# Sparse attention followed by a Fourier mix, one core: three of the four parts of a block sum added by the transfers

## The chip, the cores and the metric

The kernel runs on one core of one Trainium2 chip. Times are device microseconds of a whole execution. A profile is one further execution, recorded instruction by instruction; its span runs from the first to the last instruction, and a little of the execution's own time lies around it.

## The reference

There are 4 batches of 768 positions. The first half is an attention of 8 heads with 64 columns, in which a position looks at its neighbours closer than 16 positions and at 24 summaries, one for each block of 32 positions. The second half takes the attention's output, 512 columns wide, through a Fourier mix and a feed-forward of 2048 columns.

```python
k_sum = k.reshape(B, H, nb, block, D).max(axis=3)          # block = 32, nb = 24
v_sum = v.reshape(B, H, nb, block, D).mean(axis=3)         # the block sums of this case
scores = concat(where(|i - j| < 16, scale * q @ k.T, -1e9),
                scale * q @ k_sum.T + log(block))
x = softmax(scores) @ concat(v, v_sum)                     # then (B, S, H * D)
u = x + real(fft(fft(x, axis=1), axis=2))                  # over positions, then columns
un = (u - mean(u)) / sqrt(var(u) + 1e-6)
out = u + relu(un @ w_ch1) @ w_ch2
```

## The kernel before

**Stages.** All batches go through attention, Fourier mix and the two products with w_ch1 and w_ch2. Batch 0's attention stands alone at the start (`first_attention`, an order written out by hand for TensorE and VectorE). After it come batch 0's Fourier mix and normalisation, batch 1's attention and the conversion of the weights, interleaved by `drive`, which advances several generators in turn. The weights arrive as 64-bit floating point words and are turned into 32-bit ones by `convert` (lines 1096 to 1116: an exponent and a mantissa part, with two steps on ScalarE between VectorE's), and `make` adds the sums that the later products need. From about 80 us on, the hidden products of batch 0 run (`gen_hidden`, lines 1377 to 1410), each in pieces named hx, hy and hz whose results VectorE and ScalarE gather into h.

**The order.** Outside the hand-written part, a scheduler orders each engine's instructions by its own estimate of when they become ready, by the priorities that `drive` passes along and by `issue_after` marks. The order is fixed in the built program: each engine works through its own list, and an instruction that has to wait holds up all behind it. SyncE issues the plain transfers (`fetch`) and, through eight semaphores used in turn, each of its transfers waits until the eighth before it has landed.

**The block sums.** `block_sums(b, gg)` prepares the sums of four heads: 4 x 24 = 96 rows, one for each head and block, of 32 positions x 64 columns. For batches after the first, a row is loaded in four pieces of 8 positions, 96 x 512 values or 192 KB each, into four buffers `vb`. `add_later_blocks` adds the four pieces together; then, for batch 1, one reduction over the 8 positions that are left gives `vbs` (96 x 64). `scale_sums` multiplies it on TensorE with a table that picks the rows (vs, line 817), for two heads at a time. Batch 1 does the additions on VectorE (`tt`), later batches on GpSimd (`gtt`).

For the first four heads of batch 1, (b, gg) = (1, 0), the loads are issued in `finish_pair`, inside the hand-written part, and the additions stand behind it:

```python
            if g == NP - 2:
                block_sums(1, 0)
                load(1, 1)
...
    with tc.manual_schedule(engines={mybir.EngineType.PE, mybir.EngineType.DVE}):
        first_attention()
    add_later_blocks(1, 0)
```

**Names that follow.** qk (line 726) are the transposed keys and queries of batch 1, sc the scores with the neighbours (793), ss with the block maxima km (811, km made at 700), p the exponentials (800), av the products with the values (829, 834). x<-mx (571) adds the Fourier mix to x, bst and both (1306, 1307) are its statistics, norm (1319 to 1331) the square roots, big or un the normalised rows (1276, 1279), unt their transposes (1349), u their copies with the sums that the products need. Line 571 is the helper `tt` of nearly all of VectorE's additions, line 551 that of `fetch`, line 574 that of `gtt`. `turned` and `xr` (958, 959) are the only transfers that GpSimd issues; they belong to the Fourier mix of the last two batches.

Of the kernel before, what the change touches and what calls it, by code (L numbers as in the profile page):

```python
# [488 lines left out]
def _main_program(ctx, tc, q, k, v, moe_w_ch1, moe_w_ch2, out):  # L489


    nc = tc.nc
# [19 lines left out]
    ADD, SUB = ALU.add, ALU.subtract  # L512
# [36 lines left out]
    def fetch(out, in_):  # L549

        ins = nc.sync.dma_start(out=out, in_=in_)
        if in_order[0]:
            tc.keep_in_program_order(ins)
        return ins.ins
# [18 lines left out]
    def gtt(out, in0, in1, op):  # L573
        return nc.gpsimd.tensor_tensor(out=out, in0=in0, in1=in1, op=op).ins
# [25 lines left out]
    def room(name):  # L600
        return bpool.tile([P, NC * 2 * S], FP, tag="room", name=name)
# [12 lines left out]
    def block_sums(b, gg):  # L614

        heads, rows = slice(4 * gg, 4 * gg + 4), 4 * nb
        f = BLOCK // 4
        n = f * D
        vb = spool.tile([rows, D], FP, tag="vbs", bufs=2, name=f"vbs_{b}_{gg}")
        for g in (2 * gg, 2 * gg + 1):  # L620
            sums[b, g] = vb, sel[:, g % 2]
        src = v[b, heads].rearrange("h (n f) d -> (h n) (f d)", f=BLOCK)
        if b == 0:

            raw = words[0:rows, 4 * n * gg:4 * n * (gg + 1)]
            fetch(out=raw, in_=src)
            to_add[gg] = raw, vb
            return
        if done_weights:
            raw = room(f"vb_{b}_{gg}")  # L630
            raw = [raw[0:rows, n * i:n * (i + 1)] for i in range(4)]
        else:

            raw = [bpool.tile([P, NC, P], FP, tag="s", bufs=5, name=f"vb_{b}_{gg}_{i}").rearrange("p n t -> p (n t)")
                   [0:rows] for i in range(4)]
        for i in range(4):
            fetch(out=raw[i], in_=src[:, n * i:n * (i + 1)])
        to_add[b, gg] = raw, vb
        if (b, gg) != (1, 0):
            add_later_blocks(b, gg)  # L640

    def add_later_blocks(b, gg):
        f = BLOCK // 4
        raw, vb = to_add[b, gg]
        add = gtt if b > 1 else tt
        add(raw[0], raw[0], raw[1], ADD)
        add(raw[2], raw[2], raw[3], ADD)
        add(raw[0], raw[0], raw[2], ADD)
        if b == 1:
            nc.vector.tensor_reduce(out=vb, in_=raw[0].rearrange("p (f d) -> p d f", d=D), op=ADD, axis=AX.X)  # L650
            return
        while f > 2:
            f //= 2
            gtt(raw[0][:, 0:f * D], raw[0][:, 0:f * D], raw[0][:, f * D:2 * f * D], ADD)
        gtt(vb, raw[0][:, 0:D], raw[0][:, D:2 * D], ADD)
# [195 lines left out]
    def first_attention():  # L851
# [8 lines left out]
        def finish_pair(g):  # L860
            wide_values(0, g, p[g], x)
# [3 lines that stand above are left out]
            load_values(*following(0, g, 2))  # L865
# [125 lines left out]
    def gen_attention(b):  # L991
# [6 lines left out]
        if b > 1:  # L998
            yield
            yield  # L1000
            with tc.issue_after(marks["load"]):
                block_sums(b, 0)
            for _ in range(2):
                yield
        for g in range(NP + 1):
# [33 lines left out]
            if g == 1 and b > 1:  # L1039
                block_sums(b, 1)  # L1040
# [467 lines left out]
    for vw in vw_bufs:  # L1508
        nc.gpsimd.tensor_copy(out=vw[:, :, D].rearrange("p (e n) -> p e n", e=2),
                              in_=count[:, None, :].to_broadcast([P, 2, NQ]))  # L1510
# [26 lines left out]
# [3 lines that stand above are left out]
    fetch(out=near, in_=dr["near"].ap().rearrange("p (h i) c -> p h i c", h=2))  # L1540
    fetch(out=half_of, in_=dr["half"].ap())
# [92 lines left out]
```

## Time and profile before

| | us |
|---|---|
| three runs: median, lowest, highest | 793.76, 792.52, 799.07 |
| the profiled execution | 790.53 |
| its span | 788.6 |
| TensorE busy in the span | 776.1 |
| VectorE busy in the span | 491.2 |
| ScalarE, GpSimd busy | 224.1, 49.2 |

The granted TensorE clock of the profiled execution is 0.999 on average. A row of a timeline gives the start in us from the span's start, the time in us from the first start to the last end, the engine (PE is TensorE, DVE VectorE, ACT ScalarE, POOL GpSimd), the line, the operation, what it writes and reads, the shapes, how many instructions are merged in the row, and in brackets how long the engine had stood idle before it and what ended that. Instructions that follow each other on an engine overlap a little, so the distance from one start to the next is what a row costs. A row of a table by stretches gives the stretch, its length, the busy time with the number of instructions, the granted clock, the DMA engines' busy share and the GB/s moved. A DMA share may pass 1, since a packet's time counts where it starts.

### The profile page before, as it was taken

The page shows a single profiled execution, that of the slowest core. Times are in us where ns is not written, and L with a number is a line of the kernel's source. Part 1 is how long each engine was busy: PE and PEld are TensorE (multiplying, and loading weights), DVE is VectorE, ACT ScalarE, POOL GpSimd, SP SyncE. Part 2 cuts the span into 40 slices and gives each one's busy share as a digit, 9 for nine tenths or more (in the row PEclk, how much of TensorE's full clock was granted, in tenths as well). Part 3 has the DMA queues.
Part 4 walks back from the last instruction along what each step waited for, and adds up shares of the span by engine and source line. Part 5 has one row for each costly group of instructions (what it writes and reads, how often), then busy time and mean ns, then how long its engine had stood idle before and what let it go on. Part 6 is the DMA issues. An engine that isn't in the chain of part 4 may idle for free.

```text
span 788.6 us, 14351 instructions
## 1 busy us (share of the span) xinstructions
PE 776.1 (98%) x5920; PEld 562.9 (71%) x5920; DVE 491.2 (62%) x1017; ACT 224.1 (28%) x491; POOL 49.2 (6%) x87
## 2 busy tenths in 40 slices
PE   9999999999999999999999999999999999999997
PEld 6778455445588866787578866788569865886686
DVE  5899978697889566652759545552667623533352
ACT  3565656236536022100236012200136012001200
POOL 0000000000000030200310020300220000000000
PEclk9999999999999999999999999999999999999999
DMA  9999887796855279965442169611513163106001
GB/s 214 184 266 237 206 275 196 242 260 221 232 161 155 49 231 261 204 103 177 154 144 87 54 209 212 184 55 31 223 44 134 54 220 134 47 0 234 0 28 57
DMA packets 133353, 121.82 MB, mean 154 GB/s; under 512 B 94464, under 2 KB 114912, under 8 KB 133088
## 3 DMA queue, kind: packets, MB, share of 16 engines
q1 hardware_dynamic: 132160, 118.53, 53.9%
q0 software_dynamic: 576, 2.10, 0.8%
q8 instruction: 48, 0.79, 0.4%
q10 hardware_dynamic: 544, 0.20, 0.1%
q14 instruction: 25, 0.20, 0.1%
HBM read 97.22 MB, written 23.59 MB: 153 GB/s over the span
## 4 chain that ended last, share of the span: by engine, by line
PE 87%; DVE 9%; ACT 1%; issue 1%; DMA 1%; POOL 0%; SPq 0%; DVEq 0%; POOLq 0%
PE hx L1377 19%; PE ox L1446 18%; PE hz L1377 10%; PE oz L1446 9%; PE hy L1377 5%; PE oy L1446 5%; PE o L1423 4%; PE y L1258 3%; PE sc L793 2%; PE mx L1217 2%; PE av L829 1%; PE av L834 1%; PE qk L718 1%; DVE x L571 1%; PE unt L1349 1%
## 5 line engine op out<-in xcount | busy, mean ns | idle before, releaser
L1377 PE MATMUL hx<-u,w 128*128 128x384 f32 x512 | 185.4, 491 | 1.5 <-ACT h L1394 0.7
L1377 PEld LDWEIGHTS hx<-u,w 128*128 128x128 f32 x512 | 94.9, 190 | 70.3 <-ACT p L800 3.8
L1377 PE MATMUL hz<-u,w 128*128 128x384 f32 x256 | 93.7, 487 | 0.2 <-DVE u L571 0.2
L1446 PE MATMUL oz<-w,s 128*128 128x256 f32 x336 | 81.3, 380 | 0.0
L1446 PE MATMUL ox<-w,s 128*128 128x256 f32 x336 | 80.1, 380 | 0.0
L1446 PE MATMUL ox<-w,h 128*128 128x256 f32 x336 | 79.6, 381 | 0.0
L571 DVE TENSOR_TENSOR x<-ox,x 128x256 f32<-128x256 f32 x84 | 35.5, 423 | 66.2 <-PE ox L1446 65.9
L1377 PEld LDWEIGHTS hz<-u,w 128*128 128x128 f32 x256 | 48.4, 190 | 34.1 <-DVE u L571 0.8
L1446 PEld LDWEIGHTS ox<-w,h 128*128 128x128 f32 x336 | 63.1, 190 | 10.8 <-issue 1.2
L1446 PEld LDWEIGHTS oz<-w,s 128*128 128x128 f32 x336 | 63.3, 190 | 8.9 <-DVE x L571 0.4
L1446 PEld LDWEIGHTS ox<-w,s 128*128 128x128 f32 x336 | 63.2, 190 | 9.0 <-DVE x L571 0.3
L1388 ACT COPY h<-hx 128x384 f32<-128x384 f32 x32 | 15.3, 479 | 187.1 <-PE hx L1377 187.1
L571 DVE TENSOR_TENSOR h<-hy,h 128x384 f32<-128x384 f32 x32 | 17.8, 557 | 48.4 <-PE hy L1377 48.2
L1377 PE MATMUL hy<-u,w 128*128 128x384 f32 x128 | 46.8, 487 | 0.6 <-DVE h L571 0.6
L571 DVE TENSOR_TENSOR h<-hx,h 128x384 f32<-128x384 f32 x32 | 17.8, 556 | 44.1 <-PE hx L1377 43.9
L1423 PE MATMUL o<-w,h 128*128 128x512 f32 x96 | 42.3, 595 | 0.7 <-DVE w L571 0.7
L1407 ACT ACTIVATE h<-hx 128x384 f32<-128x384 f32 x32 | 15.7, 490 | 88.3 <-PE hx L1377 88.2
L1446 PE MATMUL oy<-w,h 128*128 128x256 f32 x168 | 40.1, 380 | 0.0
L571 DVE TENSOR_TENSOR x<-oz,x 128x256 f32<-128x256 f32 x42 | 17.8, 424 | 30.4 <-PE oz L1446 30.1
L1377 PEld LDWEIGHTS hy<-u,w 128*128 128x128 f32 x128 | 24.1, 190 | 16.9 <-DVE h L571 0.7
L1446 PEld LDWEIGHTS oy<-w,h 128*128 128x128 f32 x168 | 31.8, 190 | 4.4
L1423 PEld LDWEIGHTS o<-w,h 128*128 128x128 f32 x96 | 18.0, 190 | 22.7 <-issue 20.7
(167 smaller groups left out, 1072.8 us busy)
## 6 DMA issues: line engine op xcount, KB each, us to landing
w<-dw SPq DMA_DIRECT2D x44, 896.0 KB, 5.7
words<-in_moe_w_ch_dram SPq DMA_DIRECT2D x32, 512.0 KB, 5.7
dw<-w SPq DMA_DIRECT2D x12, 896.0 KB, 7.5
vw<-in_v_dram SPq DMA_DIRECT2D x47, 192.0 KB, 6.1
out_dram<-x SPq DMA_DIRECT2D x23, 256.0 KB, 2.0
vb<-in_v_dram SPq DMA_DIRECT2D x24, 192.0 KB, 6.8
kn<-in_k_dram SPq DMA_DIRECT2D x9, 384.0 KB, 6.1
qn<-in_q_dram SPq DMA_DIRECT2D x9, 384.0 KB, 7.6
```

The costliest lines, as they stand in the source:

```text
L571: return nc.vector.tensor_tensor(out=out, in0=in0, in1=in1, op=op).ins
L718: nc.tensor.matmul(ps[D * e:D * (e + 1), s:S2:HT], src[:, e, h, s, :], ident, start=True, stop=True)
L793: ins = nc.tensor.matmul(ps[h][r:r + 64, i, :], kt[rows, o:o + 64], qt[rows, o:o + BLOCK], start=True, stop=True)
L829: nc.tensor.matmul(av[r][32 * j:32 * (j + 1), t, :], p[rows, h, i - NB2 * h, :], vw[rows, i, :], start=(t == 0), stop=False, skip_group_ch ...
L834: ins = nc.tensor.matmul(av[r][:, t:t + HT + 1:HT, :], pm[rows, P * t:P * (t + 1)], vs[rows], start=False, stop=(t == HT - 1), skip_group_ ...
L1217: nc.tensor.matmul(out, y[:, g], table, start=False, stop=True, skip_group_check=True)
L1258: nc.tensor.matmul(y, fgs[b][par][:, st, P * g:P * (g + 1)], fs[par][:, g % 2, st, :], start=(st == 0), stop=(st == n - 1))
L1377: ins = nc.tensor.matmul(ps, w[:, a, kk, :], u[:, r, kk, :], start=start and kk == 0, stop=stop and kk == 1, skip_group_check=True)
L1388: nc.scalar.copy(out=c11, in_=X)
L1407: nc.scalar.activation(out=c21, in_=X, func=AF.Relu)
L1423: nc.tensor.matmul(ps, h[:, n, hf, P * t:P * (t + 1)], wt[2, b, j][:, 2 * hf:2 * hf + 2, :], start=(n, hf) == (0, 0), stop=(n, hf) == (NC ...
L1446: nc.tensor.matmul(ps, left[a][:, n, :], wt[2, b, j][:, r, :], start=start and n == 0, stop=stop and n == NC - 1, skip_group_check=True)
```

## The change

For (b, gg) = (1, 0) alone, SyncE loads only the first piece. The other three are transfers issued by GpSimd that add their values onto the first buffer (`accum_op=ADD`), and `add_later_blocks` leaves out the three additions; the reduction stays on VectorE. Each of the three transfers waits for the one before. All other block sums stay as they were.

```diff
-        for i in range(4):
-            fetch(out=raw[i], in_=src[:, n * i:n * (i + 1)])
+        if (b, gg) == (1, 0):
+            fetch(out=raw[0], in_=src[:, 0:n])
+            for i in range(1, 4):
+                nc.gpsimd.dma_start(out=raw[0], in_=src[:, n * i:n * (i + 1)], accum_op=ADD)
+        else:
+            for i in range(4):
+                fetch(out=raw[i], in_=src[:, n * i:n * (i + 1)])
...
-        add(raw[0], raw[0], raw[1], ADD)
-        add(raw[2], raw[2], raw[3], ADD)
-        add(raw[0], raw[0], raw[2], ADD)
+        if (b, gg) != (1, 0):
+            add(raw[0], raw[0], raw[1], ADD)
+            add(raw[2], raw[2], raw[3], ADD)
+            add(raw[0], raw[0], raw[2], ADD)
```

## The prediction

> **What bounds the kernel now.** First the head of the page, then TensorE's busy time in 20 us stretches, to see how much idle time there is to win and where.
>
> ```profile
> span 788.6 us, 14351 instructions
> PE 776.1 (98%) x5920; PEld 562.9 (71%) x5920; DVE 491.2 (62%) x1017; ACT 224.1 (28%) x491; POOL 49.2 (6%) x87
> ...
> 60.00:80.00 20.00, 19.05 (x388) 1.00 1.02 242
> 80.00:100.00 20.00, 18.69 (x216) 1.00 0.86 212
> 100.00:120.00 20.00, 20.00 (x113) 1.00 0.84 265
> ```
>
> TensorE is the bound. From 60 to 240 us its busy time falls 4.34 us short of the clock, after 240 us by about 0.4 us up to the tail. In 60 to 100 us, the only stretch where the added block sums can matter, 2.26 us are missing (0.95 + 1.31). So no relief of VectorE brings more than about 4 us, half a per cent; a loss has no such ceiling.
>
> Then VectorE's timeline where the three additions stand, with the rows around them:
>
> ```profile
> 53.25 0.70 DVE L1096 TENSOR_SCALAR words<-words 128x1024 int32<-128x1024 int32 x1 [0.62 <-DMA words<-in_moe_w_ch_dram]
> ...
> 54.62 0.69 DVE L571 TENSOR_TENSOR vb<-vb,vb 96x512 f32<-96x512 f32 x1
> 55.23 1.22 DVE L1112 SCALAR_TENSOR_TENSOR words<-words 128x1024 int32<-128x1024 int32 x1
> 56.36 0.68 DVE L571 TENSOR_TENSOR vb<-vb,vb 96x512 f32<-96x512 f32 x1
> 56.96 1.22 DVE L1114 SCALAR_TENSOR_TENSOR w<-words,w 128x1024 f32<-128x1024 uint32 x1
> 58.10 0.68 DVE L571 TENSOR_TENSOR vb<-vb,vb 96x512 f32<-96x512 f32 x1
> 59.27 0.69 DVE L571 TENSOR_TENSOR x<-mx,x 128x512 f32<-128x512 f32 x1 [0.49 <-PE mx L1299]
> 59.87 1.02 DVE L650 TENSOR_REDUCE vbs<-vb 96x64 f32<-96x512 f32 x1
> ...
> 63.20 0.68 DVE L571 TENSOR_TENSOR x<-mx,x 128x512 f32<-128x512 f32 x1
> ```
>
> VectorE is full here, and the chain of waits runs through it from 59.27 to 95.5 us: batch 0's normalisation, the transposed u and the weight conversions. TensorE just keeps up with it, out of attention work. Its timeline shows where the two touch: the transposes at 70.64 start as ScalarE's normalised tile (69.89, 0.82 long) ends, and the hy product at 95.55 waits 0.56 us for VectorE's h.
>
> ```profile
> 70.64 1.62 PE L1349 MATMUL unt<-ident,big 128*128 128x128 f32 x12
> ...
> 95.55 1.56 PE L1377 MATMUL hy<-u,w 128*128 128x384 f32 x4 [0.56 <-DVE h L571]
> ```
>
> Last, the only transfers that GpSimd issues in this kernel, which show what a serial pair costs:
>
> ```profile
> 360.21 0.87 POOL L958 DMA_DIRECT2D turned<-x  x1 [36.54 <-DVE x L571]
> 367.45 1.06 POOL L959 DMA_INDIRECT xr<-turned,mirror  x1 [6.38 <-DMA turned<-x]
> ...
> 520.37 0.75 POOL L958 DMA_DIRECT2D turned<-x  x1 [20.59 <-DVE x L571]
> 524.37 1.03 POOL L959 DMA_INDIRECT xr<-turned,mirror  x1 [3.26 <-DMA turned<-x]
> ```
>
> By the tile's view these 512 KB took 3.2 us from issue to landing on quiet DMA engines and 6.3 us with the engines' share at 0.41 to 1.18 while it ran; each time GpSimd issued the dependent transfer 0.8 to 0.9 us after the landing.
>
> **What the Trainium skill says.** "DMA: Bandwidth & Descriptors", Rules for kernel authors: an accumulating DMA reads its destination and writes it later, and nothing holds the bytes between, so each must wait for the earlier one's semaphore. The changed program has these waits; no run here shows an accumulation. The same page, Anatomy of one DMA: about 2.0 us fixed plus bytes / 436e3. For 512 KB that gives 3.2 us, which is the quiet row above; for 192 KB an estimate of 2.45 us. The same page, Queues, rings and completion order: the rings of two queues share the DMA engines packet by packet, which agrees with 6.3 us beside traffic.
>
> **The change, part by part.**
>
> *Removed from VectorE:* three additions, 0.61, 0.60 and 0.68 us from start to next start: 1.9 us.
>
> *Removed from SyncE:* three of four issues (2.39 us for four). Each SyncE transfer waits for the eighth before it, so kn, qn, vw, near and the next words go out up to about 6 us earlier. None of these is waited for between 54 and 100 us now, so I cost it at nothing; but the DMA engines will be as full from 54 to 66 us as the 0.84 share that they show there, or fuller.
>
> *Added to GpSimd:* three transfers, each waiting for the one before, the first for the plain piece. GpSimd has nothing else to do until its product p at 71.31; the third is issued before 70 us at any price below, so what is queued behind it loses nothing. DMA bytes are unchanged; each accumulation also reads its destination.
>
> *When the sum is ready.* The plain piece is issued at 40.63 and lands 13.2 us later, at 53.8: the queue ahead of it is unchanged. Each link is 0.8 us of GpSimd's reaction and L from issue to landing: T = 53.8 + 3 x (0.8 + L) = 56.2 + 3L. L lies between 2.45 us (the skill's price) and 6.3 us (the contested 512 KB store). Quiet, 3.2 us less 1.4 us of data movement in that store leaves 1.8 us fixed; 192 KB beside full queues adds about 1.2 to 2 us, the addition unknown. I take L = 3.6, T = 67.0.
>
> *When VectorE wants it.* In the changed program the reduction stands later: behind the whole w conversion, x<-mx of tile 2 and one batch-norm aggregate. With the rows' durations: 54.46 L1109 done, 55.17 (ScalarE's exponents) + 1.13 + 1.14 + 1.13 = 58.6, x<-mx at 59.27 as now (TensorE sets it), then 0.6 + 0.33 + 0.6 + 0.6 + 0.6 + 0.1 + 0.33 + 0.6 + 0.6 + 0.1 gives 63.7. If the sum is there, the batch's normalisation ends about 1.0 us earlier than the 69.86 of now: 0.7 us at its start, 0.33 us of w that stood inside it. If not, VectorE stands still, and behind the reduction in its queue wait the statistics, norm, un, and through them TensorE's transposes: its lag is -1.0 + (T + 0.1 - 63.7) = +2.4 us. Nothing absorbs it: VectorE is full to 100 us, and the transposes at 70.64 have no slack.
>
> *What the new order does later.* The instructions move well past the edit. In VectorE's queue the addition h<-hy of hidden block 0, now at 94.94, comes behind the w2 conversion. From the reciprocal at 88.50 its end is: 0.24 (two reciprocals) + 0.94 + 0.93 + 5.87 (w1: 0.60 + 0.60 + 1.14 + 1.13 + 1.13 + 0.34 + 0.60 + 0.33) + 4.60 (w2, without sums) + 0.86 + 0.55 = 14.0, so 102.5 instead of 95.5. TensorE's second hy product still waits for it. TensorE has taken other work forward: from 93.1, 2.26 of av, two hx groups of 1.49, 1.88 of sc and 0.2 of ss, so it arrives at 100.4 without stalls. Now the same work with its 0.56 us stall would be done at 101.0. TensorE loses 102.6 - 101.0 = 1.6 us, plus VectorE's lag. Walked on to 120 us I find no further stall in either order.
>
> *Sum.* 1.6 + 2.4 = +4.0 us. The stall at the transposes is inside it, not beside it: both are the same lag of VectorE. Against the profiled execution, 790.53 us (span 788.6 and 1.9 around it), that is 794.5; it lies 3.2 us below the median of the runs, so against the median 793.76 it is 797.8.
>
> **The rivals.**
>
> *Hidden chain.* L at or below 2.5 us: T is at most 63.7, nothing waits, VectorE is 1.0 us ahead, and 1.6 - 1.0 = +0.6 us remains: 794.4. For: 2.45 us by the skill's price. Against: the DMA engines are nearly full here.
>
> *Slower by over 1%.* The chain's landings under load, at the reduction on VectorE. At L = 6.3 T is 75.1, the lag +10.5, the total +12.1: 805.9. It passes 1% (7.9 us) from L = 4.9 on. For: the contested store; 3475 packets under 512 B pass the engines from 54 to 66 us; the addition itself is unpriced. Against: the store is 2.7 times as large.
>
> *VectorE's relief counts.* The order costs nothing because my walk mistakes which wait comes last, and the stalls of 60 to 100 us go: 2.26 and some tenths later, -2.6 us, 791.2. For: 1.9 us of work is gone from a full engine. Against: the hy wait.
>
> **How the numbers follow.** Forecast (L from 2.5 to 4.9) 0.52; hidden chain 0.15; slower by over 1% 0.20; relief 0.13, of which 0.02 for a gain over 1%, which TensorE's idle time forbids. About 1%, 7.9 us, is what a measurement of this kernel can tell from no change; the runs before spread by 0.8%. The first, the second and the rest of the fourth fall within it: 0.78. The range runs from 793.0, just below the hidden chain, to 805.0, L = 6.0; about 0.2 lies outside.
>
> **What would show it.** Right: GpSimd's three transfers some 4.4 us apart from 54.6; the reduction beginning at 67 with a wait of about 3 us for a DMA; the first un transposes at 73; the hy product waiting about 2 us for VectorE's h. Wrong: a reduction without a wait (hidden chain), gaps of 7 us between the transfers (slower), or the hy product in time although VectorE is late.

## The result and the profile after

The changed kernel takes 801.71 us, median of runs from 799.89 to 805.39, against 794.27 us for the kernel before on the same chip (792.34 to 799.07). The ratio is 1.0098, 95% interval 1.0070 to 1.0127: 7.8 us slower by the ratio (7.4 between the medians), just under 1%, with an interval that reaches past 1%. It lies inside the range of the prediction, 3.9 us above the predicted time. The profiled execution took 805.39 us and is the longest of the changed kernel's; the profile of before is of a short one (790.53 us). So the two profiles lie twice as far apart as the medians, and the shares below are read stage by stage. When the scores (sc) ahead of the transposes start, this execution is 1.96 us behind the profile of before (71.06 against 69.10 us).

The head of the page, and TensorE's table by stretches (length, busy time, granted clock, DMA share, GB/s):

```profile
span 803.5 us, 14349 instructions
PE 779.2 (97%) x5920; PEld 564.9 (70%) x5920; DVE 491.9 (61%) x1014; ACT 224.6 (28%) x491; POOL 51.8 (6%) x90
```

```profile
60.00:80.00 20.00, 12.66 (x154) 0.93 1.09 224
80.00:100.00 20.00, 18.20 (x271) 0.73 0.46 139
100.00:120.00 20.00, 19.20 (x249) 1.00 1.04 267
```

TensorE had 19.05 us of work between 60 and 80 us; now it has 12.66. Between 80 and 100 us it is busy again, but at a granted clock of 0.73: part of that work is slower work, not more work.

GpSimd's timeline, VectorE's reduction and TensorE's transposes, from the changed kernel's trace:

```profile
55.69 1.05 POOL L639 DMA_DIRECT2D vb<-in_v_dram  x1 [10.99 <-DMA vb<-in_v_dram]
62.83 0.81 POOL L639 DMA_DIRECT2D vb<-in_v_dram  x1 [6.10 <-DMA vb<-in_v_dram]
69.57 0.79 POOL L639 DMA_DIRECT2D vb<-in_v_dram  x1 [5.93 <-DMA vb<-in_v_dram]
...
75.30 1.01 DVE L656 TENSOR_REDUCE vbs<-vb 96x64 f32<-96x512 f32 x1 [9.58 <-DMA vb<-in_v_dram]
...
81.46 2.82 PE L1355 MATMUL unt<-ident,big 128*128 128x128 f32 x12 [8.81 <-DVE big L1285]
```

The three transfers follow each other after 7.14 and 6.74 us, and the last lands 5.7 us after its issue. VectorE stands still for 9.58 us, with the statistics and norm queued behind the reduction, and TensorE stands still for 8.81 us ahead of the transposes. Those twelve transposes then take 2.82 us where they took 1.62: the granted clock is 0.50. TensorE's stretches once more, cut where the clock changes:

```profile
60.00:77.30 17.30, 12.66 (x154) 1.00 1.08 216
77.30:91.00 13.70, 9.54 (x218) 0.50 0.52 132
91.00:100.00 9.00, 8.66 (x57) 1.00 0.57 191
```

### The profile page after: what moved, and what is told of

Its sections match the earlier page's. It is cut to its first block, busy times and chain, and to the rows that moved or that the text cites. A ratio compares the mean times of both kernels' runs of the same rounds, so it can differ in the third digit from the quotient of the medians.

```text
span 803.5 us, 14349 instructions
## 1 busy us (share of the span) xinstructions
PE 779.2 (97%) x5920; PEld 564.9 (70%) x5920; DVE 491.9 (61%) x1014; ACT 224.6 (28%) x491; POOL 51.8 (6%) x90
## 4 chain that ended last, share of the span: by engine, by line
PE 83%; DMA 7%; DVE 5%; ACT 2%; issue 1%; SPq 0%; DVEq 0%
PE hx L1383 18%; PE ox L1452 18%; PE oz L1452 9%; PE hz L1383 9%; PE o L1429 5%; PE oy L1452 5%; PE hy L1383 5%; DMA vb<-in_v_dram 4%; PE y L1264 2%; PE sc L799 2%; DMA qn<-in_q_dram 2%; PE mx L1223 2%; PE av L835 1%; PE unt L1355 1%; PE av L840 1%; PE ss L817 1%
## 5 line engine op out<-in xcount | busy, mean ns | idle before, releaser
L1452 PEld LDWEIGHTS ox<-w,h 128*128 128x128 f32 x336 | 63.1, 190 | 10.8 <-issue 1.2
```

The lines of the kernel that those rows point to most:

```text
L1452: nc.tensor.matmul(ps, left[a][:, n, :], wt[2, b, j][:, r, :], start=start and n == 0, stop=stop and n == NC - 1, skip_group_check=True)
```

## The experiments

Two theories stood against each other at first. In the first, the chain of three transfers lands late and everything follows from VectorE's wait. In the second, the moved instructions cost a good part, as the prediction held with its +1.6 us. Behind the first stood a question: what makes a link 6 to 7 us long?

**Without the chain, in the same order.**

```diff
-            for i in range(1, 4):
-                nc.gpsimd.dma_start(out=raw[0], in_=src[:, n * i:n * (i + 1)], accum_op=ADD)
...
-    add_later_blocks(1, 0)
...
-                    nc.vector.bn_aggr(out=both[:, i], in_=bst)
+                    agg = nc.vector.bn_aggr(out=both[:, i], in_=bst)
+                    if t == 1:
+                        with tc.issue_after(agg.ins):
+                            add_later_blocks(1, 0)
```

> The changed kernel without GpSimd's three transfers (three quarters of the values are left out of the sum); the reduction is held at its place, so VectorE, TensorE, ScalarE and SyncE work through the same lists as in the changed kernel. Chain theory (the late sum costs everything): the reduction at about 63 us without a wait, the transposes at 70 to 71, no drop of the granted clock, time 792.5 to 796 against 794.3 before (ratio 0.998 to 1.002). Order theory (the moved instructions cost a good part, +1.6 us as predicted or more): 796 to 799, with TensorE waiting at the hy product near 100 us.

Measured: 793.28 us, ratio 0.9999 (0.9982 to 1.0015). On VectorE, then on TensorE:

```profile
67.28 1.01 DVE L654 TENSOR_REDUCE vbs<-vb 96x64 f32<-96x512 f32 x1
...
74.23 1.53 PE L1356 MATMUL unt<-ident,big 128*128 128x128 f32 x12
...
80.10 0.31 PE L797 MATMUL sc<-qt,kt 64*64 64x32 f32 x5 [1.68 <-issue]
```

No wait at either, and the transposes run at the full clock. (This execution lies 3.6 us later than the profile of before at this point: sc starts at 72.70 us.) By the times, the whole loss is the chain's. The row also shows that there was nothing to win: VectorE's list is 1.9 us shorter and its norm does end 0.7 us earlier relative to x<-mx, but the transposes start exactly as long after sc as before (1.53 against 1.54 us), because sc stands ahead of them in TensorE's list. The time is that of the kernel before, within 1.4 us. The last row shows a stop that has nothing to do with the sum: in the next sc, after 91 of its 96 products, TensorE stands still for 1.68 us, held by nothing that the profile shows, and from 80.9 to 84.3 us the clock is 0.50. The profiles of before and of the changed kernel have these 96 products without a gap.

**Writing instead of adding.**

```diff
-                nc.gpsimd.dma_start(out=raw[0], in_=src[:, n * i:n * (i + 1)], accum_op=ADD)
+                nc.gpsimd.dma_start(out=raw[0], in_=src[:, n * i:n * (i + 1)])
```

> The three GpSimd transfers write instead of add (only the last piece is summed), still each after the one before; all lists of instructions are the same. If the addition inside the transfer is what makes a link 5.7 to 6.8 us long: links of 3 to 4.5 us, reduction at 66 to 70, time 795 to 798. If the length comes from what surrounds the transfer (full DMA engines, shared rings, issuing): links of 5.5 to 7 us again, reduction at 74 to 76, time 800 to 803 (ratio 1.007 to 1.012).

Measured: 801.34 us, ratio 1.0085 (1.0056 to 1.0114), reduction at 73.65 us after a wait of 9.61 us. The line's view gives the time from issue to landing:

```profile
DMA to landing us min/median/max: 6.4/7.0/7.7
```

In the changed kernel the same line reads 5.7/6.5/6.8. The addition isn't what makes the links long; here they are even longer without it. Nor is it VectorE working beside them: in the changed kernel VectorE stands still through the whole third link, and that one still takes 5.7 us.

**Small pieces.**

```diff
-                nc.gpsimd.dma_start(out=raw[0], in_=src[:, n * i:n * (i + 1)], accum_op=ADD)
+                nc.gpsimd.dma_start(out=raw[0][:, 0:64], in_=src[:, n * i:n * i + 64], accum_op=ADD)
```

> Each of the three accumulating transfers brings 96 x 64 values (24 KB) instead of 96 x 512 (192 KB); the rest of the three pieces is left out of the sum. If the bytes beside full DMA engines are the price: links of 2 to 3 us, the sum ready at 62 to 65 us, no wait at the reduction, time as without the chain (793 to 796). If a fixed part (issue to first packet, completion, waiting behind other queues' packets) is the price: links of 4.5 us or more, reduction at 70 to 73, time 797 to 800.

Measured: 802.54 us, ratio 1.0100 (1.0070 to 1.0131). GpSimd's and VectorE's timelines:

```profile
55.01 1.05 POOL L639 DMA_DIRECT2D vb<-in_v_dram  x1 [11.68 <-DMA vb<-in_v_dram]
61.18 0.80 POOL L639 DMA_DIRECT2D vb<-in_v_dram  x1 [5.12 <-DMA vb<-in_v_dram]
66.01 0.79 POOL L639 DMA_DIRECT2D vb<-in_v_dram  x1 [4.03 <-DMA vb<-in_v_dram]
...
72.01 1.01 DVE L656 TENSOR_REDUCE vbs<-vb 96x64 f32<-96x512 f32 x1 [9.19 <-DMA vb<-in_v_dram]
```

An eighth of the bytes saves little more than a tenth of the links, 6.17, 4.83 and 6.00 us. The time is above what either theory expected, and VectorE's wait is hardly shorter, because the order changed too: the reduction stands a few rows earlier in VectorE's list and begins to wait at 62.82 us, not at 65.72. GpSimd's list, and with it the chain, is the same. So neither adding nor moving the bytes is the main price in this stage. It is something that each transfer meets at either size.

**Links by themselves.** The kernel before, with a chain of thirty transfers onto a buffer that is no longer used (`near`, behind the last attention).

```diff
+            spare = near.rearrange("p h i c -> p (h i c)")[0:96, 0:512]
+            with tc.issue_after(marks["fold", 3]):
+                nc.gpsimd.memset(spare, 0.0)
+                for k in range(30):
...
+                    if k % 3 == 0:
+                        nc.gpsimd.dma_start(out=spare, in_=one, accum_op=ADD)
+                    elif k % 3 == 1:
+                        nc.gpsimd.dma_start(out=spare, in_=one)
+                    else:
+                        nc.gpsimd.dma_start(out=spare[:, 0:64], in_=one[:, 0:64], accum_op=ADD)
```

> The kernel before with a chain of thirty GpSimd transfers of no use after its last attention: in turn one that adds 96 x 512 values, one that writes as many, one that adds 96 x 64, each waiting for the one before, partly on idle DMA engines (from about 570 us on), partly beside other loads. If the links of 6 us come from the surroundings, links on idle engines take 2 to 3 us and longer ones appear only beside traffic. If the addition or the way through GpSimd is that slow by itself, links of 5 us or more stay there on idle engines. The 96 x 512 forms against the 96 x 64 form show what the bytes cost, adding against writing what the addition costs.

GpSimd's timeline; L1587 adds 96 x 512, L1589 writes 96 x 512, L1591 adds 96 x 64. Then the table by stretches for the third to the fifth of these links:

```profile
542.25 0.80 POOL L1587 DMA_DIRECT2D near<-in_v_dram  x1 [1.73 <-DMA near<-in_v_dram]
546.03 0.54 POOL L1589 DMA_DIRECT2D near<-in_v_dram  x1 [2.99 <-DMA near<-in_v_dram]
549.10 0.79 POOL L1591 DMA_DIRECT2D near<-in_v_dram  x1 [2.52 <-DMA near<-in_v_dram]
551.57 0.79 POOL L1587 DMA_DIRECT2D near<-in_v_dram  x1 [1.68 <-DMA near<-in_v_dram]
557.65 0.54 POOL L1589 DMA_DIRECT2D near<-in_v_dram  x1 [5.30 <-DMA near<-in_v_dram]
564.87 0.78 POOL L1591 DMA_DIRECT2D near<-in_v_dram  x1 [6.67 <-DMA near<-in_v_dram]
```

```profile
549.10:551.30 2.20, 0.79 (x1) 1.00 0.13 11
551.60:557.40 5.80, 0.76 (x1) 1.00 0.74 204
557.70:564.60 6.90, 0.50 (x1) 1.00 1.01 386
```

The one execution took 816.82 us; it is not compared, since the thirty links lengthen its end. From start to next start: on idle engines 3.78 us to add 192 KB, 3.07 us to write it, 2.47 us to add 24 KB. The next add and the next write of the same sizes take 6.08 and 7.22 us, while other transfers fill the DMA engines to a share of 0.74 and 1.01. In medians over the chain, issue to landing is 3.5, 2.7 and 2.3 us; the longest ones are 5.8 and 6.9 us, both beside traffic. These are as long as the changed kernel's links. On idle engines, by the starts, the bytes cost 1.3 us and the addition 0.7 us. Beside traffic the add takes 2.3 us more and the write 4.2; the 24 KB link right behind them, at a share of 0.79, takes 3.44 us, only 1.0 more. With the run before, where 24 KB took 4.83 to 6.17 us, a link beside other traffic costs 1 to 4 us more than on idle engines, and its size alone doesn't decide how much. The Trainium skill, "DMA: Bandwidth & Descriptors", Anatomy of one DMA, gives an estimate of 2.45 us for 192 KB. Written on idle engines this trace has 2.7, so the estimate comes within a tenth there; beside other transfers, with 6.9, it does not hold.

Up to 519 us this run works through the same lists as the kernel before, so it is also a second profile of it. Here that kernel stops inside the same sc, after the same 91 products:

```profile
76.89 0.31 PE L793 MATMUL sc<-qt,kt 64*64 64x32 f32 x5 [1.01 <-issue]
```

From 77.2 to 80.6 us the clock is 0.50. So the stop does not come from the changed order; the profile of before is of an execution without it.

**Less traffic.** The four loads of vw for the first two heads of batch 1 are left out.

```diff
-            for h in range(2):
+            for h in range(0 if (b, g) == (1, 0) else 2):
```

> The changed kernel without the four loads of vw for the first two heads of batch 1 (768 packets of 256 B each; old values stay there, so a part of batch 1's attention is computed from other values). They are most of the small packets beside the first links. If the traffic of small packets makes the links long: the first two links 3 to 4.5 us, the reduction waits 4 to 6 us instead of 9.6, time 796 to 799. If the length is in the GpSimd transfer itself: links of 5 to 7 us, wait 8 to 10 us, 800 to 803.

Measured: 809.69 us, ratio 1.0187 (1.0155 to 1.0219), above what either theory expected. The links did not shorten (6.6/7.2/7.3 us), and the reason is in the table by stretches of the three links:

```profile
54.00:60.60 6.60, 1.04 (x1) 1.00 1.06 299
60.90:68.10 7.20, 0.80 (x1) 1.00 1.32 186
68.40:75.70 7.30, 0.78 (x1) 0.99 1.02 248
```

The DMA share stayed above 1. SyncE's list moved up and its next transfers took the place of the ones that were gone. So this run doesn't tell which traffic lengthens the links, only that taking these loads away did not empty the engines. It also has another order of instructions (VectorE's from 60 us on, TensorE's from 95), and VectorE waits 11.25 us; its 8 us over the changed kernel were not taken apart.

**A filled wait.** Ten products of no use just ahead of the transposes.

```diff
+                if b == 0 and t == 0:
+                    keep_busy(10, fd.rearrange("p a n -> p (a n)"))
```

> The changed kernel with ten products of no use (128x512, about 0.86 us each, 8.6 us in all) on TensorE just ahead of the transposes it waits for. VectorE's list is the same up to the copies of u. If the half clock after the idle costs its own 3 to 4 us: the wait for the sum stays at 9 to 10 us, the granted clock stays at 1.00, the twelve transposes take 1.6 us instead of 2.8, and the time is 797 to 799 (ratio 1.005 to 1.007). If the clock costs nothing in the end, because other waits take its place: 801 to 803 as with the change.

Measured: 806.39 us, ratio 1.0164 (1.0136 to 1.0192). The wait on VectorE stayed at 9.59 us and the clock stayed at 1.00 up to 87.8 us. TensorE's timeline:

```profile
81.09 1.49 PE L1357 MATMUL unt<-ident,big 128*128 128x128 f32 x11 [0.76 <-ACT p L806]
...
91.31 2.01 PE L835 MATMUL av<-vw,p 64*32 64x65 f32 x96 [6.05 <-issue]
```

The transposes do run at full clock, but then av waits 6.05 us, and the time is above what either theory expected. ScalarE's list explains it: with the ten products in its estimates the scheduler put the next normalised tile (85.64, after a wait of 4.64 us for VectorE's norm) and a weight conversion (L1103 and L1116, from 87.28 us on) ahead of ScalarE's copies of the transposes (89.28), the exponentials of ss (90.70) and the scaled sums (91.08); av needs the last two. The experiment changed two things at once, so what the half clock costs by itself stays a reading of rows: the five groups from unt to av take 9.47 us in the changed kernel and 5.74 us before, 3.7 us more.

**Two short chains.**

```diff
-            for i in range(1, 4):
-                nc.gpsimd.dma_start(out=raw[0], in_=src[:, n * i:n * (i + 1)], accum_op=ADD)
+            fetch(out=raw[2], in_=src[:, 2 * n:3 * n])
+            for i in (0, 2):
+                nc.gpsimd.dma_start(out=raw[i], in_=src[:, n * (i + 1):n * (i + 2)], accum_op=ADD)
...
+        add(raw[0], raw[0], raw[2], ADD)
```

> Two plain pieces by SyncE, onto each of them one accumulating transfer, both in flight together; VectorE adds the two halves (one addition instead of three). Chain theory: the depth of the chain decides, so with one link of 6 to 7.5 us the halves are there at 62 to 65 us, the wait on VectorE is 0 to 4 us instead of 9.6, time 793 to 798 (ratio 0.998 to 1.005). If any GpSimd transfer in this stage costs (contention, issuing), 799 or more.

Measured: 794.70 us, ratio 1.0015 (1.0002 to 1.0028). The two transfers land 6.9 and 8.3 us after their issue, each slower than the three of the changed kernel's profile, and still VectorE waits only 1.77 us. The depth decides here, not the price of one transfer. What is left of the wait shows something else on TensorE:

```profile
72.04 2.62 PE L1356 MATMUL unt<-ident,big 128*128 128x128 f32 x12 [1.39 <-DVE big L1286]
```

Behind a wait of only 1.39 us the clock is 0.50, from 72.5 to 75.9 us.

**The chain started early, and the same without the chain.** The block sums' loads are issued with the first pair of batch 0 instead of the third, with the reduction held at its place as in the first experiment; then the same with GpSimd's three transfers taken out.

```diff
             if g < NP - 2:
+                if g == 0:
+                    block_sums(1, 0)
                 finish_pair(g)
...
             if g == NP - 2:
-                block_sums(1, 0)
                 load(1, 1)
```

> The changed kernel with the plain piece issued some 17 us earlier on SyncE (near 26 us), the reduction held at its place. Chain theory: the plain piece lands at 36 to 40 us, three links of about 6.5 us make the sum ready at 55 to 60, the reduction doesn't wait, no drop of the clock, and the time is that without the chain, 792 to 796 (ratio 0.998 to 1.003): the change can be repaired, but gains nothing. If the transfers cost something where they are, the early ones delay the loads of the first attention and the time is 797 or more.

> The kernel with the early plain piece, without GpSimd's three transfers (three quarters of the values are left out of the sum); TensorE, VectorE, ScalarE and SyncE work through the same lists as with the early chain, which stood at a ratio of 1.0039. If those 3 us are the moved instructions (the hy product that waits 1.3 us for h, and the half clock after it): again 1.003 to 1.005, 796 to 797.5, with the same wait at hy near 104 us. If they are the transfers themselves, which fill the DMA engines from 32 to 50 us: 0.998 to 1.001, 792 to 794.5.

Measured: with the early chain 796.68 us, ratio 1.0039 (1.0022 to 1.0055); without it 795.44 us, ratio 1.0022 (1.0008 to 1.0035). Both lie between what the theories expected. With the chain GpSimd issues at 32.24, 37.01 and 42.32 us (55.69 to 69.57 in the changed kernel), and the reduction at 64.02 us waits for nothing: starting the chain early takes away more than half of the loss. Of the rest, 0.22% is there without the transfers too, from the order or from the plain piece that is loaded earlier; what the transfers add, 0.17%, is smaller than the two intervals can separate. One difference between the two traces is a place where the order's wait meets the clock. TensorE's timelines, with the early chain and then without:

```profile
104.28 1.65 PE L1387 MATMUL hy<-u,w 128*128 128x384 f32 x2 [1.28 <-DVE h L571]
```

```profile
103.55 0.91 PE L1385 MATMUL hy<-u,w 128*128 128x384 f32 x2 [0.60 <-DVE h L571]
```

In the first the clock is 0.50 from 103.7 to 110.5 us, in the second it stays at 1.00. Two thirds of a microsecond more of waiting lie beside 6.8 us at half speed. Both traces also have a wait of 1.4 to 1.5 us for p, which ends at about 101.8 us. Whether the difference repeats from one execution to the next was not tried.

**The change once more.**

> The changed kernel once more, for a second profile of it: the first is of its longest execution. Chain theory: links of 5.5 to 7.5 us, a wait of 8 to 10 us at the reduction, the half clock behind it for 7 to 14 us, time 800 to 803 (ratio 1.007 to 1.013). If the first profile was out of the ordinary: a wait of 4 to 7 us.

Measured: 802.52 us, ratio 1.0094 (1.0065 to 1.0122). The second profile has the same picture: landings of 5.3/7.3/7.8 us, a wait of 9.04 us on VectorE, 8.27 us on TensorE, and a clock of 0.50 for 13.7 us. The first was not out of the ordinary.

No version here beats the kernel before. The run without the chain has all three additions taken from VectorE for nothing and is no faster, so in the changed kernel's order of instructions no cheaper way of adding the pieces could have won anything.

## Why the prediction was right and where it was wrong

The predicted class came true: no difference over 1%, though only just, and that was in part luck. The direction was right, the size was short by 3.9 us, and the mechanism was nearer to the rival that it put at 0.20 than to its own forecast: with the landing as measured, its own terms give 8.7 + 1.6 = 10.3 us, over 1%. Step by step, with the 1.96 us by which this execution ran late taken off:

- **When VectorE wants the sum:** 63.7 predicted, 65.72 - 1.96 = 63.8 measured. Right, including the instructions that the new order puts ahead of the reduction.
- **The plain piece:** landing 53.8 predicted, 55.4 - 1.96 = 53.4 measured; GpSimd acts on it at 55.69 - 1.96 = 53.73. Right.
- **GpSimd's reaction:** 0.8 us taken from the pairs at 360 and 520 us, about 0.3 measured (the first link lands at 62.5, the next is issued at 62.83). Three times 0.5 us too much.
- **L, the step that failed:** 3.6 us taken, 6.8, 6.5 and 5.7 measured. The estimate put 1.2 to 2 us for the bytes beside full queues on a fixed part of 1.8 us. The sum is what such a link costs on idle engines (3.5 us alone); the part of the surroundings, 2.8 us in the mean, was missing from it. A number that includes this part was on the page of before. Its list of DMA issues (KB of one, median us to landing) has a row for just these pieces of 192 KB:

```profile
vb<-in_v_dram SPq DMA_DIRECT2D x24, 192.0 KB, 6.8
```

  Those are SyncE's transfers, and four of them are issued together, so they wait partly for each other. But the row was nearer to this link than the 512 KB transfer of a quieter stage, and it says what a transfer of this size costs in this kernel beside its usual traffic. The prediction used that transfer's 6.3 us only as a bound, and argued it down because the transfer was 2.7 times as large; small pieces took 4.5 to 6.0 us in this stage, so size was no argument.
- **T, the sum:** 67.0 predicted; 75.30 - 1.96 = 73.3 measured.
- **The lag carried through:** with this T the prediction's own formula gives -1.0 + (73.4 - 63.7) = +8.7 us at the transposes, 70.64 + 8.7 = 79.3. Measured: 81.46 - 1.96 = 79.5. The path from the reduction through norm to TensorE was right, and so was the claim that nothing absorbs it.
- **The order, +1.6 us:** the end of h<-hy was put at 102.5; without the chain it comes at 106.1 - 3.6 = 102.5. TensorE nevertheless did not wait for it, because it came to hy at 107.10 - 3.6 = 103.5, not at 100.4. It was 1.3 us late already at av, where the working starts, after the stop inside sc; and its walk held a wait of 0.64 us for ScalarE's p and one of 0.61 us in a later sc that the working lacked. So the missing wait at hy says little about this term. Order and head start together were put at +0.6 us and measured at -0.1 us (-1.4 to +1.2). The run can't separate these; with the early loads and no chain, where hy does wait 0.60 us, order and earlier plain piece together measure +0.22%, 1.7 us.
- **SyncE's transfers up to 6 us earlier, at nothing:** with the 1.96 us taken off, kn, qn, vw and near go out 0.9, 3.4, 1.9 and 2.0 us earlier. The shift is there, smaller, and in neither trace does an engine wait for these loads in this stage.
- **The clock:** not in the prediction at all. It treated a stall of TensorE as its own length. The Trainium skill, "TensorE: Matmul & The Clock Gate", Part 1 on the clock gate, says that the array falls to half speed after an idle window of about 3.4 us and that the window runs free. The traces agree: the half clock lasts 3.4 us with the two short chains, 6.8 us with the early one and 13.7 us here, about one, two and four windows; the two half-clock stretches of the early chain's trace begin 27.3 us apart (76.4 and 103.7), eight windows; and here the 3.4 us before the drop, 73.9 to 77.3, hold no product at all. The half clock adds 3.7 us of rows behind a wait of 8.8 us.

Wait and clock together are 12.5 us; the waits of 0.82 us and less that stood behind the transposes before are gone, and at the end of the two profiles 12.9 us remain (803.5 - 1.96 - 788.6). The medians differ by 7.4 us. The 5.5 us between these lie in the choice of executions: the profile of before is 3.7 us below its median of 794.27, and the changed kernel's is 1.7 us further above its own than the 1.96 us explain.

A part of this can be named. The stop inside sc and the half clock behind it, which the profile of before lacks, are in the second profile of that kernel and in the three without a wait at the transposes. From the start of the first sc to the second group of transposes the profile of before takes 8.0 us, these four 10.2 to 10.8 us, and the two of the changed kernel, which don't have the stop, 20.6 and 19.8 us. Against an execution with the stop the change costs 9 to 10.4 us there, not about 12. What causes the stop, how often it comes, and what else sets these executions apart stay open.

The rival "slower by over 1%" named the place, the chain's landings at the reduction, and its deciding point, L of 4.9 us, was passed with 6.3 in the mean. Its +12.1 us stand close to the 12.9 of the two profiles, with other terms: the reaction and the order too dear, the clock missing. By the medians the loss stays just under its 1%. The hidden chain and the relief of VectorE both fell: the first needed links of 2.5 us, less than they take even on idle engines, and the second had nothing to win at the transposes. The prediction read their start at 70.64 us as the end of ScalarE's normalised tile (70.71); but sc, ahead of them in TensorE's list, ended then as well (70.70).

## What to carry to other kernels

Price a new transfer by the row of the page that shows the same size beside the same traffic, not by its cost on idle engines. A chain of dependent transfers pays the crowded engines' waiting once for each link, so count the depth before the bytes: here two transfers side by side, one link deep, cost a wait of 1.8 us where three in a row cost 9.6. And before moving work off an engine, look at what stands ahead of the waiting instruction in the next engine's list: the norm came 0.7 us earlier and the transposes did not move.

## What was unexpected of the hardware

In the chain beside full DMA engines a 24 KB transfer of GpSimd took 4.5 to 6.0 us from issue to landing and a 192 KB one 5.3 to 7.8 us; on idle engines they took 2.3 and 3.5 us. Here the crowd costs more than the size.

A short wait can be followed by half the clock. With the two short chains it was 1.39 us without work, behind 1.6 us of small products (64x32); with the stop inside sc it was 1.0 to 1.9 us, in four profiles. Each time one window of 3.4 us at 0.50 followed. The skill's page puts the drop after an idle window; here it came after windows with up to 2.4 us of work in them. A wait of 1.42 us for p, in the profile with the early loads and no chain, had no such drop behind it. What decides, these traces don't tell.
